# Strassen's form for the second product of a fused Fourier mixing and SoLU block, with its sums on GpSimd

## The chip, the core and the metric

The kernel runs on one core of a Trainium2 chip. Times are device microseconds (us) of one execution. The kernel before took 1793.22 us (median of four executions, 1790.22 to 1795.94; the prediction had the first three of them, with 1792.19). Traces come from one profiled execution each; every profiled run used here is of the state "fast", so no disturbed clock enters the comparison.

Engine names as the profile has them: PE is TensorE (matmuls), PEld its weight loads, DVE is VectorE, ACT is ScalarE, POOL is GpSimd, SP is SyncE, which here only issues transfers. A name such as L486 is a line of the kernel that the view belongs to; the same statement has another line number in another kernel.

## The reference, cut to what matters

```python
X = np.fft.rfft(x, axis=1)                       # x: (8, 3136, 256)
y = np.fft.irfft(X * (filt_r + 1j*filt_i)[None], n=3136, axis=1)
x = y.reshape(25088, 256)
h = x @ w_in                                     # 256 -> 1024
e = np.exp(h - h_max);  sm = e / (sum(e) + 1e-9)
solu = h * sm
ln = (solu - mu) / np.sqrt(var + 1e-6) * g_ln
out = ln @ w_out                                 # 1024 -> 256
```

The transform of 3136 points is done in matmuls (49 x 64 points with twiddles between). The 25088 tokens are 196 blocks of 128. The mean of `ln` is folded into `w_out`, and its division by the deviation becomes a scale per row at the very end.

## The kernel before: what the change and the argument touch

The loop makes one step for each block of 128 tokens; two steps are a pair of blocks. The first product `h = x @ w_in` is already in Strassen's form over a pair: seven products instead of eight, on 128x128 sums that GpSimd makes one pair ahead.

```python
def pair_sums(j):                                     # GpSimd, 128 x 128
    sums[j] = s = wk2.tile([P, 4, P], FP32, ...)      # two buffers
    # ... a11 to a22: the four 128x128 parts of the pair's input
    tt = nc.gpsimd.tensor_tensor
    tt(out=s[:, 0, :], in0=a21, in1=a22, op=ALU.add)
    tt(out=s[:, 1, :], in0=s[:, 0, :], in1=a11, op=ALU.subtract)
    tt(out=s[:, 2, :], in0=a11, in1=a21, op=ALU.subtract)
    tt(out=s[:, 3, :], in0=a12, in1=s[:, 1, :], op=ALU.subtract)

def normalize(k):                                     # VectorE, two inputs of 128 x 1024 in SBUF
    # ...
    nc.vector.scalar_tensor_tensor(out=solu, in0=e, scalar=rsum, in1=solu,
                                   op0=ALU.mult, op1=ALU.mult, accum_out=nmu)
    # ... then ScalarE squares it for the variance
```

The normalised block is transposed in 32x32 pieces on VectorE and regrouped by four DMAs (`solu_t<-turn`). The projection is plain: eight matmuls of 256 columns per block, then one scaled eviction by VectorE.

```python
def project(k, ps, half):
    # ...
    for f in range(KF // 2 * half, KF // 2 * half + KF // 2):
        nc.tensor.matmul(out=ps, lhsT=solu_ts[divmod(k, 4)][:, f, :], rhs=w_out_sb[:, f, :], ...)

def scale(k, ps):
    # ...
    nc.vector.tensor_scalar(out=ot, in0=ps, scalar1=rss[g][:, a:a + 1], scalar2=None, op0=ALU.mult)
    # ...
    nc.sync.dma_start(out=rows[a], in_=ot)
```

Beside the token work runs the transform of the later images: rows are loaded (`r`), a first matmul makes `pa`, ScalarE copies it to `t1`, which goes to DRAM as `d1`; it comes back as `t2`, is multiplied with the twiddle table and the filter (`pb`, `p`, `i`, `pc`, `g`), goes to DRAM as `d2`, comes back into the same row buffers `r` and gives `y` (`py`). In the trace `d<-t` is the store of `t1`, and `t<-d` is either of the two loads back. The buffers for this:

```python
pools = {name: pool(name + "1", bufs)
         for name, bufs in (("r", 4), ("t1", 2), ("t2", 3), ("p", 2), ("g", 2))}
# ...
# a row load is issued when the row buffer four loads back is free:
at = max(t - 3, row_loads[n - 4][0] if n >= 4 else -1)
```

## Time and profile before

| of the kernel before | value |
|---|---|
| median time | 1793.22 us |
| span of the profiled run, mean clock | 1795.5 us, 0.988 |
| TensorE busy, share | 1721.1 us, 96% |
| VectorE, ScalarE, GpSimd busy | 64%, 55%, 40% |
| two-input instruction of `normalize` | 196 x 1308 ns |
| 128x128 sums on GpSimd | 392 x 579 ns (median 458) |

The share of busy time is no measure of the room that is left, since records of pipelined matmuls overlap: those of the projection last 379 ns on average and start 216 ns apart. I therefore use one account throughout. Each TensorE record gets the spacing at which records of its shape follow one another when nothing is in the way: 429 ns for 512 columns, 216 for 256 and 110 for 98 (about their mean; the median is 112). Their sum is what TensorE needs; the span less that sum is stall, whatever its reason. A pair begins with its product 1 of the first layer. For the kernel before that is 1672.4 us needed and 123.1 us of stall. Of the stall, 78.1 us come before the first pair of blocks, 28.5 in pairs 0 to 18 (up to 520 us), 7.9 in pairs 18 to 97 and 8.6 at the end. From pair 18 on, this kernel has next to no room to give.

What TensorE waited for is in the view of waits of the profile of the kernel before, for PE alone; its columns are the waiting instruction, what released it, total us, number and longest:

```profile
PE pa L176 <- DMA x<-in_x_dram: 21.3, 9, 6.9
...
PE m L464 <- ACT h L474: 7.5, 5, 4.9
PE pb L205 <- DMA de<-de_tbl: 4.9, 5, 2.0
...
PE py L260 <- DMA t<-d: 1.6, 2, 0.8
...
PE py L260 <- ACT t L179: 0.9, 1, 0.9
PE po L549 <- DVE h L512: 0.8, 1, 0.8
```

And from the groups of its page, the two-input instruction of `normalize` (count, then busy us and mean ns, then idle time before it):

```profile
L512 DVE SCALAR_TENSOR_TENSOR h<-e,rsum,h 128x1024 f32<-128x1024 f32 x196 | 256.4, 1308 | 7.1 <-DMA x<-in_x_dram 0.3
```

No line names GpSimd (POOL); the only wait for VectorE which the list holds outside the transform is 0.8 us.

### The profile page before, as it was taken

How to read it: one execution, taken by the hardware profiler on the slowest of the kernel's cores; microseconds unless marked ns; L12 is line 12 of the kernel's file. 1: busy time of each engine (PE TensorE's matmuls, PEld its weight loads, DVE VectorE, ACT ScalarE, POOL GpSimd, SP SyncE). 2: the span in 40 equal slices, each digit the busy share in tenths (PEclk: the TensorE clock that was granted, in tenths of full speed). 3: DMA queues.
4: the chain of work that ended last, by engine and by line, in shares of the span. 5: the costliest groups of instructions: out<-in, count | busy, mean ns of one | idle time of the engine just before them, and what ended most of it. 6: DMA issues, size and time to landing. Idle time of an engine off the chain costs nothing.

```text
span 1795.5 us, 22752 instructions
## 1 busy us (share of the span) xinstructions
PE 1721.1 (96%) x6324; PEld 1112.1 (62%) x6324; DVE 1155.9 (64%) x2370; ACT 990.9 (55%) x1623; POOL 718.8 (40%) x1698
## 2 busy tenths in 40 slices
PE   6589889999999999999999999999999999999998
PEld 2125455566666666766666666676777677666666
DVE  0794545567666665677777655667676766677773
ACT  2265555566666655566666555555655555555452
POOL 3242544465455543335445333344443332324331
PEclk9699999999999999999999999999999999999999
DMA  9786789987799765577667565567775444433334
GB/s 270 250 258 191 217 224 247 246 215 205 207 232 222 191 184 145 151 167 199 180 174 203 142 162 146 127 170 191 191 188 133 107 120 108 107 103 104 102 96 119
DMA packets 323180, 313.98 MB, mean 175 GB/s; under 512 B 26465, under 2 KB 284514, under 8 KB 323056
## 3 DMA queue, kind: packets, MB, share of 16 engines
q1 hardware_dynamic: 292496, 219.79, 48.3%
q0 software_dynamic: 28768, 86.45, 16.6%
q10 hardware_dynamic: 1792, 6.29, 1.0%
q8 instruction: 53, 0.87, 0.2%
q14 instruction: 71, 0.58, 0.1%
HBM read 131.55 MB, written 81.40 MB: 119 GB/s over the span
## 4 chain that ended last, share of the span: by engine, by line
PE 83%; DMA 9%; DVE 3%; ACT 2%; issue 1%; POOL 1%; SPq 1%; DVEq 0%; ACTq 0%; POOLq 0%
PE po L549 35%; PE m L464 30%; PE py L260 6%; PE pa L176 4%; PE pc L235 4%; PE pb L205 4%; DMA x<-in_x_dram 3%; DMA d<-t 2%; DMA t<-d 2%; DMA de<-de_tbl 1%; DVE p L226 1%; DVE p L224 1%; PE idle L370 1%; DMA solu_t<-turn 0%; DVE i L225 0%
## 5 line engine op out<-in xcount | busy, mean ns | idle before, releaser
L549 PE MATMUL po<-w_out_sb,solu_t 128*128 128x256 f32 x3136 | 724.5, 379 | 2.4 <-DMA solu_t<-turn 1.6
L549 PEld LDWEIGHTS po<-w_out_sb,solu_t 128*128 128x128 f32 x3136 | 593.3, 190 | 190.0 <-issue 114.9
L464 PE MATMUL m<-w_in_sb,sums 128*128 128x512 f32 x784 | 399.1, 600 | 7.5 <-ACT h L474 7.5
L514 ACT ACTIVATE e<-h,nmu 128x1024 f32<-128x1024 f32 x196 | 225.1, 1149 | 223.3 <-DVE h L512 219.5
L464 PE MATMUL m<-w_in_sb,y 128*128 128x512 f32 x588 | 286.8, 597 | 0.1
L474 ACT COPY h<-m 128x512 f32<-128x512 f32 x294 | 172.4, 586 | 176.6 <-PE m L464 162.9
L512 DVE SCALAR_TENSOR_TENSOR h<-e,rsum,h 128x1024 f32<-128x1024 f32 x196 | 256.4, 1308 | 7.1 <-DMA x<-in_x_dram 0.3
L488 DVE CUSTOM_DVE_ANT_0 h<-m,h 128x512 f32<-128x512 f32 x196 | 133.9, 683 | 173.3 <-ACT h L474 86.0
L243 POOL DMA_DIRECT2D d<-g x101 | 77.2, 764 | 416.0 <-ACT g L238 407.0
L522 DVE STREAM_TRANSPOSE turn<-h 128x1024 f32<-128x1024 f32 x196 | 242.2, 1236 | 0.4 <-DVE ot L558 0.3
L496 ACT ACTIVATE e<-h,nmax 128x1024 f32<-128x1024 f32 x196 | 225.8, 1152 | 0.1
L558 DVE TENSOR_SCALAR ot<-po,rs_t 128x256 f32<-128x256 f32 x196 | 94.3, 481 | 171.6 <-issue 84.9
L464 PEld LDWEIGHTS m<-w_in_sb,sums 128*128 128x128 f32 x784 | 141.3, 190 | 96.0 <-issue 72.6
L541 POOL COPY rs_t<-rs 32x1 f32<-32x1 f32 x784 | 181.6, 232 | 35.7
L464 PEld LDWEIGHTS m<-w_in_sb,y 128*128 128x128 f32 x588 | 109.7, 191 | 112.7 <-issue 92.5
L224 DVE TENSOR_TENSOR p<-pb,f 128x512 f32<-128x512 f32 (+1 forms) x101 | 69.1, 685 | 149.9 <-ACT i L217 147.5
L176 PE MATMUL pa<-x,wf_t 98*100 98x512 f32 x256 | 138.3, 649 | 25.8 <-DMA x<-in_x_dram 21.3
L260 PEld LDWEIGHTS py<-wi_t,t 100*128 100x128 f32 x1024 | 131.7, 192 | 50.1 <-issue 31.5
L263 ACT COPY y<-py 128x392 f32<-128x392 f32 x128 | 108.2, 846 | 85.8 <-PE py L260 84.8
L179 ACT COPY t<-pa 100x512 f32<-100x512 f32 (+1 forms) x112 | 71.8, 646 | 133.5 <-PE pa L176 109.9
L260 PE MATMUL py<-wi_t,t 100*128 100x98 f32 x1024 | 132.0, 273 | 2.6 <-DMA t<-d 1.6
L205 PE MATMUL pb<-t,de 128*128 128x512 f32 (+1 forms) x250 | 108.1, 532 | 19.4 <-DMA t<-d 11.5
(65 smaller groups left out, 1441.4 us busy)
## 6 DMA issues: line engine op xcount, KB each, us to landing
solu_t<-turn SPq DMA_DIRECT2D x784, 128.0 KB
t<-d SPq DMA_DIRECT2D x99, 256.0 KB
d<-g POOLq DMA_DIRECT2D x99, 256.0 KB, 4.4
out_dram<-ot SPq DMA_DIRECT2D x196, 128.0 KB
x<-in_x_dram SPq DMA_DIRECT2D x64, 384.0 KB
t<-d SPq DMA_DIRECT2D x64, 384.0 KB
d<-t POOLq DMA_DIRECT2D x48, 384.0 KB, 5.8
f<-f_dram POOLq DMA_DIRECT2D x104, 128.0 KB, 5.7
```

The lines of the kernel that those rows point to most:

```text
L176: nc.tensor.matmul(out=ps[0:NK, j], lhsT=wf_t, rhs=self.xs[i][0:NR, 2 * u:2 * u + 2, :], start=True, stop=True)
L205: nc.tensor.matmul(out=ps[:, w * j:w * j + w, :], lhsT=self.des[i][:, j, 0, :], rhs=t2[:, w * j:w * j + w, :], start=True, stop=True)
L260: nc.tensor.matmul(out=psv[:, i, :], lhsT=t4s[e, ch][:, i, cb * P:cb * P + P], rhs=wi_t, start=True, stop=True)
L464: nc.tensor.matmul(out=ms[j, bank], lhsT=lhsT, rhs=w_in_sb[:, w, :], start=m in (1, 2, 7), stop=True, skip_group_check=True)
L474: nc.scalar.copy(out=h_half(k, i), in_=ms[j, 0])
L488: nc.vector.tensor_tensor_reduce(out=h_half(k, i), in0=ms[j, bank], in1=h_half(*kept), scale=1.0, scalar=sofar, op0=ALU.add, op1=ALU.min, ...
L496: nc.scalar.activation(out=e, in_=hs[k], func=AFT.Exp, bias=nmaxs.pop(k)[:, 1:2], scale=-1.0, accum_out=esum)
L512: nc.vector.scalar_tensor_tensor(out=solu, in0=e, scalar=rsum, in1=solu, op0=ALU.mult, op1=ALU.mult, accum_out=nmu)
L514: nc.scalar.activation(out=e, in_=solu, func=AFT.Square, bias=nmu, scale=-float(DFF), accum_out=variances[g][:, i:i + 1])
L522: nc.vector.transpose(out=turns[g][:, :, i, :], in_=solus.pop(k).rearrange("p (f j) -> p f j", j=32))
L541: nc.gpsimd.tensor_copy(out=rss[g][32 * i:32 * i + 32, c:c + 1], in_=rs[32 * c:32 * c + 32, i:i + 1])
L549: nc.tensor.matmul(out=ps, lhsT=solu_ts[divmod(k, 4)][:, f, :], rhs=w_out_sb[:, f, :], start=(f == 0), stop=(f == KF - 1), skip_group_chec ...
```

## The change

Its intent: the projection too is done for two blocks at once in Strassen's form. With the two blocks as rows and the halves of `DFF` as columns, seven products of four matmuls of 128 columns, 28 in all, take the place of 16 matmuls of 256 columns. The price is four sums of 128x512 per pair on GpSimd, and more, smaller evictions. Three things come with it: the weight combinations of `w_out` make that tile 14 KB per partition instead of 8, the sums need 8 KB more, and the buffers of the transform are cut by 10 KB to pay for it; loads of tables and spectrum rows move from SyncE's to ScalarE's queue; each row load is one transfer instead of two. Beside these, half of the tile of the small sums gets one buffer instead of two (`s23` in the kernel).

```diff
-LAG = 8
+LAG = 9
-    w_out_sb = consts.tile([P, KF, C], FP32, name="w_out_sb")
+    w_out_sb = consts.tile([P, 7, KF // 2, C // 2], FP32, name="w_out_sb")
...
-             for name, bufs in (("r", 4), ("t1", 2), ("t2", 3), ("p", 2), ("g", 2))}
+             for name, bufs in (("r", 3), ("t1", 3), ("t2", 2), ("p", 2), ("g", 2))}   # t1: half pieces
-        at = max(t - 3, row_loads[n - 4][0] if n >= 4 else -1)
+        at = max(t - 3, row_loads[n - 3][0] if n >= 3 else -1)
-            products[t].append(lambda sp=sp, i=i: sp.multiply(i))
+            products[t].append(lambda sp=sp, i=i: sp.multiply(i, bufs=1))               # one i tile
...
-            ahead(t, 3).append(lambda sp=sp, i=i: sp.fetch(i))
+            ahead(t, 2).append(lambda sp=sp, i=i: sp.fetch(i, nc.scalar.dma_start))
-        nc.sync.dma_start(out=de[:, 0:count], in_=de_dram[:, s:s + count, :, :])
+        nc.scalar.dma_start(out=de[:, 0:count], in_=de_dram[:, s:s + count, :, :])
...
+    def project_sums(p, step):
+        (a11, a12), (a21, a22) = solu_ts[p, 0], solu_ts[p, 1]
+        if step == 0:
+            s1 = upool.tile([P, KF // 2, P], FP32, name=f"u1_{p}", tag="u1")
+            sum_of(s1, a21, a22, ALU.add)
+            sum_of(a21, a11, a21, ALU.subtract)
+            solu_sums[p] = s1, None, a21, None
+        else:
+            s2 = spool.tile([P, KF // 2, P], FP32, name=f"u2_{p}", tag="u2")
+            s4 = spool.tile([P, KF // 2, P], FP32, name=f"u4_{p}", tag="u4")
...
+            sum_of(s2, s1, a11, ALU.subtract)
+            sum_of(s4, a12, s2, ALU.subtract)
...
+    def project(p, m):
...
+        for f in range(KF // 2):
+            nc.tensor.matmul(out=pos[p, bank], lhsT=lhs[:, f, :], rhs=w[:, f, :], ...)
...
...
+    def keep_out(p, i, to):          # ScalarE, scaled copy of a product that two outputs share
+    def finish_out(p, i, n, kept, bank):   # VectorE, 128 columns, adds the kept one
```

In the order of the step, `project_sums(j - 3, 0)` stands after products 3 and 4 of the first layer in odd steps, ahead of `pair_sums(j + 1)`; `project_sums(j - 4, 1)` stands in even steps.

## The prediction

The prediction's sum came to 1792 - 62 + 4.5 + 4 + 15 = 1754 us and was shaded to 1750. Cut is the reason given for a spacing of 112 ns where streaming alone would need 108; the spacing itself is measured, 112 ns for 98 columns in the kernel before and 112 for 128 columns in the changed one. In rival (a), 1722 is 1739 with 109 ns for each of the 5488 records instead of 112, an estimate from the eight records that took 0.87 us.

"The lock" is my assumption that VectorE's two-input instruction (L512) and a sum on GpSimd hold each other up. The lines quoted for it show a sum that took 1.11 us when it started under L512, and the next one 0.46.

> **What bounds the kernel now.** I read the page first (busy shares, chain that ended last, groups), then the stretches, then instructions in order of time. From the page:
>
> ```profile
> PE 1721.1 (96%) x6324; PEld 1112.1 (62%) x6324; DVE 1155.9 (64%) x2370; ACT 990.9 (55%) x1623; POOL 718.8 (40%) x1698
> ...
> PE 83%; DMA 9%; DVE 3%; ACT 2%; issue 1%; POOL 1%; SPq 1%; DVEq 0%; ACTq 0%; POOLq 0%
> PE po L549 35%; PE m L464 30%; PE py L260 6%; PE pa L176 4%; PE pc L235 4%; PE pb L205 4%; DMA x<-in_x_dram 3%; DMA d<-t 2%; DMA t<-d 2%; DMA de<-de_tbl 1%; DVE p L226 1%; DVE p L224 1%; PE idle L370 1%; DMA solu_t<-turn 0%; DVE i L225 0%
> ...
> L549 PE MATMUL po<-w_out_sb,solu_t 128*128 128x256 f32 x3136 | 724.5, 379 | 2.4 <-DMA solu_t<-turn 1.6
> ```
>
> TensorE bounds it, and the projection (L549) is the largest item on the chain. Its 3136 records are 196 blocks x 8 matmuls x 2: an fp32 matmul shows as two pairs of load and stream. Busy time of pipelined matmuls overlaps, so I take the spacing of starts instead. Stretches of the run show where TensorE is really full:
>
> ```profile
> 0.00:100.00 100.00, 63.65 (x101) 20.40 (x102) 44.76 (x78) 33.21 (x44) 32.27 (x55) 0.85 0.86 257
> 100.00:200.00 100.00, 87.66 (x306) 44.23 (x305) 62.16 (x117) 56.16 (x89) 36.32 (x58) 0.97 0.74 224
> 200.00:300.00 100.00, 86.56 (x285) 48.24 (x284) 56.07 (x117) 58.70 (x100) 47.85 (x104) 0.97 0.85 226
> ...
> 700.00:900.00 200.00, 200.00 (x764) 133.21 (x763) 139.03 (x285) 121.20 (x198) 84.24 (x205) 1.00 0.68 171
> ...
> 1600.00:1700.00 100.00, 100.00 (x354) 66.39 (x353) 71.22 (x154) 50.44 (x85) 34.89 (x101) 1.00 0.39 102
> ```
>
> Columns: length, busy of PE, PEld, DVE, ACT, POOL, clock, DMA share, GB/s. From about 400 us on TensorE has no gap; before 300 us it idles 12 to 36 us per 100 and the DMA engines are at 0.74 to 0.86 (0.94 between 300 and 400). The spacing:
>
> ```profile
> 900.66 3.62 PE L549 MATMUL po<-w_out_sb,solu_t 128*128 128x256 f32 x16
> 904.12 1.02 PE L464 MATMUL m<-w_in_sb,sums 128*128 128x512 f32 x2
> ...
> 916.15 1.03 PE L260 MATMUL py<-wi_t,t 100*128 100x98 f32 x8
> 917.02 1.05 PE L464 MATMUL m<-w_in_sb,sums 128*128 128x512 f32 x2
> ```
>
> Sixteen records of 256 columns take 904.12 - 900.66 = 3.46 us, 216 ns each; 512 columns cost 429 ns (median of 973 spacings of L464). Eight of 98 columns take 0.87 us, 109 ns each; inside such a run the median spacing is 112 ns, although 98 columns at 256 columns' rate would stream in 83 ns. [...] This line decides the worth of the change.
>
> [...] Our sums of 128 elements have a median of 458 ns[...]. [...]
>
> ```profile
> 1652.07 1.28 DVE L512 SCALAR_TENSOR_TENSOR h<-e,rsum,h 128x1024 f32<-128x1024 f32 x1
> ...
> 1652.56 1.11 POOL L451 TENSOR_TENSOR sums<-y 128x128 f32<-128x128 f32 x1 [3.15 <-PE m L464]
> ...
> 1653.75 0.46 POOL L452 TENSOR_TENSOR sums<-sums,y 128x128 f32<-128x128 f32 x1
> ```
>
> L451 started under L512, took 1.11 us, and the next sum 0.46. [...]
>
> **The change, part by part.**
> TensorE: 3136 x 216 ns = 677 us go. Added are 98 pairs x 7 products x 4 matmuls x 2 = 5488 records of 128 columns. Streaming alone would need about 108 ns[...]; I take 112: 615 us. Gain 62 us (0.64 per pair). Not the eighth (85 us) that seven for eight promises[...]. All lies on the path, except where DMA sets the pace: the trace has 14 of the 196 blocks projected before 400 us (one begins at 381.43, the next at 397.36 us), and their 14 x 0.32 = 4.5 us I count as lost.
> GpSimd: 392 sums of 128x512 x 1.27 us = 498 us, making 1217 of some 1740. Per pair of blocks 5.1 us come to 84.24/200 x 16.5 = 6.9 us in the middle and 34.89/100 x 13.06 = 4.6 us at the end (13.06 us is the spacing of pairs there). So 12.0 of 15.9 us, and 9.7 of 12.4. Waits for the lock come on top: two L512 per pair, 2.6 us at worst. Off the path on average, but 80 to 95% of it.
> VectorE: 196 x 481 ns = 94 us go; 392 PSUM operations of 128 columns, an estimate of 347 each from the 749 of L485's 512 and the 481 of L558's 256 columns: 136 us. Net +42, plus lock waits up to 1.27 us a time.
> ScalarE: 294 copies of 128 columns, 265 ns by the line through 586 (512) and 372 (256): 78 us; and some 152 issues of 0.42 us (what SyncE takes for them) = 64. It reaches 1133 us, no bound.
> SyncE: loses those issues and the second half of each row load. Its gain is order: loads no longer queue behind a store that waits (589 us of its waits are for L558).
> End: the last pair's sums lie bare, two steps of two, 5.1 us, less what the shorter products save: +4.
> Waits newly put on TensorE: in an odd step without spectral work, TensorE needs 3 x 0.86 + 4 x 0.90 = 6.2 us. VectorE and ScalarE have a chain beside it: product 5 read by the copy (1.6 us), exponential 1.34, copy of product 1 0.3, its finish 0.35, reciprocal 0.3, L512 1.37, L485 0.8: about 6.1 us before bank 0 is free. There is no slack there for a lock wait, where before bank 0 was freed about 0.9 us early (1654.0 against 1654.9). Where spectral work is mixed in there are 3 to 4 us more of TensorE per pair. I guess 0.15 us per pair, 15 us, as a choice and not a measurement.
> Sum: 1792 - 62 + 4.5 + 4 + 15 = 1754. The row loads' release, and that the buffers look sized to keep this going, make me shade it to 1750.
>
> **Rivals.**
> (a) No new wait: 1792 - 62 + 8.5 = 1739, or 1722[...]. For it: TensorE's waits for GpSimd's sums are near nothing today. Against: the 6.1 of 6.2 us above.
> (b) GpSimd or the lock becomes the bound: a sum of 1.27 us held against L512, and the loop from product 4 over the regroup DMA (4.5 us in the end stage), two sums, the pair's own sums and product 6. That loop is about 12 us at 12.4 a pair. With 0.6 us more in each pair the gain is gone: 1795. For it: sums of 128 elements already rise from 458 to a mean of 579. Against: more work per pair in most of the run.
> (c) The stage up to 400 us is bound by DMA, and [...]fewer row buffers (4 to 3) make it longer: +10 to 15, 1765.
> (d) The smaller matmuls cost more than 112 ns[...]: at 123 ns nothing is left, 1792 or more.
>
> **Range and chances.** Between (a) at its best and half of (b): 1722 to 1785. Faster by over 2% means below 1756; the centre is near the edge, so 0.56, 0.38 and 0.06.
>
> **What would show it.** In the changed kernel's trace: the spacing of 128-column matmuls (112 expected; 123 kills it); the median of the 128x512 sums (1.27 us) and their mean (up to 1.7 under the lock); GpSimd's share near 70%; TensorE's waits for outputs m and o on VectorE or ScalarE (15 us), for the sums (under 10), and for row loads before 400 us (up to 15 more); pairs in the end stage 12.4 to 12.7 us apart instead of 13.06. The prediction is wrong if that spacing stays above 12.9[...].

## The result

The changed kernel took 1822.07 us (median of four, 1820.77 to 1824.32). It computes the right result. Ratios in this document are the mean time of one kernel's fast runs over that of the other's fast runs of the same rounds, so not quite the ratio of the medians that are quoted; here the ratio is 1.0163, with a 95% interval of 1.0141 to 1.0184. That is slower by 1.6%, where 1750 us and a range of 1722 to 1785 had been predicted. (It is within 2% of the kernel before, the middle one of the prediction's three chances, 0.38.)

From the page of the changed kernel, first the busy shares and the chain that ended last, then groups (line, engine, operation, output<-inputs, shapes, count, then busy us and mean ns, then idle time before and what ended it):

```profile
PE 1686.6 (93%) x8692; PEld 1149.0 (63%) x8692; DVE 1246.2 (69%) x2586; ACT 1069.8 (59%) x1917; POOL 1267.2 (70%) x2090
...
PE 63%; DMA 10%; DVE 9%; POOL 6%; issue 6%; ACT 4%; SPq 1%; ACTq 1%; POOLq 0%; DVEq 0%
...
L595 PE MATMUL o<-w_out_sb,solu_t 128*128 128x128 f32 x3136 | 405.1, 278 | 5.0 <-DVE ot L614 4.0
...
L534 DVE SCALAR_TENSOR_TENSOR h<-e,rsum,h 128x1024 f32<-128x1024 f32 x196 | 292.2, 1491 | 7.1 <-DVE rsum L531 0.3
...
L465 POOL TENSOR_TENSOR solu_t<-solu_t,solu_t 128x512 f32<-128x512 f32 x98 | 156.7, 1599 | 7.7
```

TensorE fell from 83% of the chain to 63%, and VectorE, GpSimd and ScalarE rose together from 6% to 19%. The two-input instruction of `normalize`, whose code did not change, takes 1491 ns on average instead of 1308; its median is still 1286, so it is a minority of instances that became much longer: 79 of 196 are over 1350 ns, against 24 before.

The same stretches of the run as those of the prediction (length, then busy us of PE, PEld, DVE, ACT, POOL with counts, clock, DMA share, GB/s), changed kernel:

```profile
200.00:300.00 100.00, 77.95 (x253) 43.70 (x254) 51.51 (x111) 50.00 (x89) 53.85 (x101) 0.85 0.66 190
...
700.00:900.00 200.00, 190.22 (x1024) 131.89 (x1023) 141.25 (x295) 126.41 (x226) 145.76 (x248) 0.99 0.60 164
1600.00:1700.00 100.00, 97.59 (x558) 70.36 (x557) 76.89 (x175) 58.20 (x111) 80.97 (x133) 1.00 0.39 101
```

TensorE now has holes in the middle too, 190 of 200 us. Between 200 and 300 us it is less busy than before, its granted clock is 0.85 instead of 0.97, and the DMA engines fell from 0.85 to 0.66: this stretch is not held by the bandwidth of transfers. The waits below show transfers that start late.

In the account by stage, in us of stall (needed time 1672.4 before, 1609.8 after):

```text
stage              before   after   difference
before pair 0        78.1    78.2     +0.1
pairs 0 to 18        28.5    64.5    +36.0    the transform of later images is dense here
pairs 18 to 70        4.3    42.4    +38.1
pairs 70 to 97        3.6     8.1     +4.5    no transform left but the last step
end                   8.6    16.0     +7.4
sum                 123.1   209.2    +86.1
```

So the saving came: 1672.4 - 1609.8 = 62.6 us. It was eaten by 86.1 us of new stall, and 86.1 - 62.6 = 23.5 us is the difference of the spans (1819.0 - 1795.5). What ended TensorE's waits, in the view of waits of the changed kernel for PE:

```profile
PE py L266 <- ACT t L185: 17.0, 4, 7.9
...
PE pb L210 <- DVE p L230: 11.8, 13, 2.9
...
PE m L486 <- DVE nmax L510: 10.6, 13, 2.8
PE pb L210 <- DMA de<-de_tbl: 9.7, 4, 3.2
...
PE m L486 <- POOL s L465: 6.9, 9, 1.4
PE o L595 <- ACT ot L607: 5.2, 8, 1.4
PE o L595 <- DVE ot L614: 4.0, 4, 1.7
```

There are two kinds. The first line is the early stage: four long waits of `py`, between 174 and 290 us. Most of the others are short waits for VectorE and for GpSimd's sums, the larger part of them after pair 18.

**The short waits.** Two extracts of the changed kernel's timeline (start, duration, engine, line, operation; in brackets the idle time before and what ended it), the first in the early stage, the second near the end:

```profile
245.42 3.31 DVE L534 SCALAR_TENSOR_TENSOR h<-e,rsum,h 128x1024 f32<-128x1024 f32 x1
246.36 1.28 POOL L465 TENSOR_TENSOR u<-u,solu_t 128x512 f32<-128x512 f32 x1
247.71 2.14 POOL L465 TENSOR_TENSOR u<-solu_t,u 128x512 f32<-128x512 f32 x1
...
248.83 1.15 ACT L536 ACTIVATE e<-h,nmu 128x1024 f32<-128x1024 f32 x1 [3.83 <-DVE h L534]
```

```profile
1644.72 1.28 DVE L534 SCALAR_TENSOR_TENSOR h<-e,rsum,h 128x1024 f32<-128x1024 f32 x1
1644.84 2.30 POOL L465 TENSOR_TENSOR u<-solu_t,u 128x512 f32<-128x512 f32 x1
...
1650.72 1.13 PE L486 MATMUL m<-w_in_sb,s 128*128 128x512 f32 x2 [0.81 <-POOL s L465]
...
1651.01 1.56 DVE L534 SCALAR_TENSOR_TENSOR h<-e,rsum,h 128x1024 f32<-128x1024 f32 x1
```

In the first, VectorE's instruction of 1.28 us takes 3.31. A sum of 1.28 us runs inside it. If VectorE stood still for all of that, which is my reading and not shown, 0.75 of the 2.03 us more stay unexplained (in its first 0.93 us GpSimd was issuing transfers). The next sum then starts under VectorE and takes 2.14. In the second VectorE was first, and the sum takes 2.30 us. Six us later a product of the first layer waits for the small sums, which stand behind the long ones in GpSimd's queue. Each of the two lengthens the other's work: 3.31 us for 1.28 on VectorE, 2.14 and 2.30 for 1.28 on GpSimd.

**The long waits.** In the timeline of the changed kernel between 282 and 292 us:

```profile
282.28 1.69 POOL L190 DMA_DIRECT2D d<-t  x3
...
289.45 0.59 ACT L185 COPY t<-pa 100x512 f32<-100x512 f32 x1 [10.17 <-DMA d<-t]
290.09 2.03 PE L266 MATMUL py<-wi_t,t 100*128 100x98 f32 x8 [7.93 <-ACT t L185]
...
291.91 3.65 PE L595 MATMUL o<-w_out_sb,solu_t 128*128 128x128 f32 x16
```

ScalarE cannot copy the next `pa`, since all its `t1` buffers wait for stores that GpSimd issued late; it stands 10.17 us, and TensorE, whose output bank (the store of sums that its products write to) ScalarE should empty, 7.93. Of the 10.17 us, some 3 pass before GpSimd issues the stores at 282.28, behind its sums. Afterwards eight matmuls of 98 columns take 2.03 us, where the prediction's lines showed eight in 1.03, and sixteen of 128 columns take 3.65 instead of 1.95. TensorE's granted clock, 1.00 from 270 to 285 us, stands at 0.50 from 285.3 to 295.3 us. The same is seen earlier: after a pause of 2.59 us `py` takes 3.73 us for 16 records, at a granted clock of 0.50 from 216.9 to 227.1 us, where the kernel before took 2.03 after a pause of 0.89. If the pause brings the clock down, it is paid twice; that is my reading of these two places, and no run tests it. In pairs 0 to 18 the granted clock is at half for 6.8 us before and 43.9 us after. Counting records at one and a half to 2.3 times their spacing as half clocked, the lost time in the whole run is an estimate of 22 to 25 us before and 39 to 51 after, by which records are counted; this is a part of the stall above, not more of it.

### The profile page after: what moved, and what is told of

Its sections match the earlier page's. It is cut to its first block, busy times and chain, and to the rows that moved or that the text cites. A ratio compares the mean times of both kernels' runs of the same rounds, so it can differ in the third digit from the quotient of the medians.

```text
span 1819.0 us, 29269 instructions
## 1 busy us (share of the span) xinstructions
PE 1686.6 (93%) x8692; PEld 1149.0 (63%) x8692; DVE 1246.2 (69%) x2586; ACT 1069.8 (59%) x1917; POOL 1267.2 (70%) x2090
## 4 chain that ended last, share of the span: by engine, by line
PE 63%; DMA 10%; DVE 9%; POOL 6%; issue 6%; ACT 4%; SPq 1%; ACTq 1%; POOLq 0%; DVEq 0%
PE o L595 24%; PE m L486 22%; PE py L266 6%; PE pa L183 3%; PE pb L210 3%; PE pc L241 3%; DVE h L534 2%; DMA de<-de_tbl 2%; DMA d<-t 2%; DMA x<-in_x_dram 2%; DMA solu_t<-turn 2%; POOL rs_t L566 2%; POOL u L465 1%; DMA t<-d 1%; DVE turn L544 1%
## 5 line engine op out<-in xcount | busy, mean ns | idle before, releaser
L486 PE MATMUL m<-w_in_sb,s 128*128 128x512 f32 x784 | 400.7, 603 | 18.4 <-ACT h L496 11.4
L595 PE MATMUL o<-w_out_sb,solu_t 128*128 128x128 f32 x3136 | 405.1, 278 | 5.0 <-DVE ot L614 4.0
L595 PEld LDWEIGHTS o<-w_out_sb,solu_t 128*128 128x128 f32 x3136 | 385.1, 195 | 35.8 <-issue 27.5
L595 PEld LDWEIGHTS o<-w_out_sb,u 128*128 128x128 f32 x2352 | 308.4, 192 | 144.6 <-issue 114.5
L595 PE MATMUL o<-w_out_sb,u 128*128 128x128 f32 x2352 | 312.6, 276 | 6.9 <-ACT ot L607 5.2
L534 DVE SCALAR_TENSOR_TENSOR h<-e,rsum,h 128x1024 f32<-128x1024 f32 x196 | 292.2, 1491 | 7.1 <-DVE rsum L531 0.3
L465 POOL TENSOR_TENSOR u<-solu_t 128x512 f32<-128x512 f32 x98 | 142.4, 1453 | 154.9 <-DMA solu_t<-turn 95.6
L614 DVE SCALAR_TENSOR_TENSOR ot<-o,rs_t,ot 128x128 f32<-128x128 f32 x294 | 101.3, 345 | 212.5 <-ACT ot L607 157.4
L465 POOL TENSOR_TENSOR u<-solu_t,u 128x512 f32<-128x512 f32 x98 | 150.7, 1537 | 59.6 <-PE o L595 54.7
L486 PEld LDWEIGHTS m<-w_in_sb,s 128*128 128x128 f32 x784 | 130.5, 193 | 96.4 <-issue 69.0
L465 POOL TENSOR_TENSOR solu_t<-solu_t,solu_t 128x512 f32<-128x512 f32 x98 | 156.7, 1599 | 7.7
```

The lines of the kernel that those rows point to most:

```text
L465: nc.gpsimd.tensor_tensor(out=out, in0=in0, in1=in1, op=op)
L486: nc.tensor.matmul(out=ms[j, bank], lhsT=lhsT, rhs=w_in_sb[:, w, :], start=m in (1, 2, 7), stop=True, skip_group_check=True)
L595: nc.tensor.matmul(out=pos[p, bank], lhsT=lhs[:, f, :], rhs=w[:, f, :], start=f == 0 and m in (1, 2, 7), stop=True, skip_group_check=True)
```

## The experiments

My theory after the traces had two parts. For pairs 18 to 97, GpSimd's sums and VectorE's two-input instructions hold each other up, as in the two extracts above (the lock, in what follows; the expectations say exclusion), and the chain from VectorE to TensorE has no slack for that. For pairs 0 to 18, the new order of work or the buffers that were given up hold the transform. Rivals: the time that the sums take in GpSimd's queue; the smaller matmuls and evictions themselves; the moved loads.

Eighteen kernels were run. Every run was also timed against the kernel before, whose medians were 1798.1, 1794.6, 1796.1, 1797.8 and 1795.4. A table of all of them stands after the last. Kernels that read something other than the sums give a wrong result; that is said with each.

### The sums: removed, unread, without reads, elsewhere

**No sums.** The products read the transposed blocks themselves (a wrong result).

```diff
 def project_sums(p, step):
     (a11, a12), (a21, a22) = solu_ts[p, 0], solu_ts[p, 1]
     if step == 0:
-        ...four sums
+        solu_sums[p] = a21, a11, a21, a12
```

> The changed kernel without the 392 sums of solu on GpSimd (the products read the unsummed halves, so the result is wrong on purpose). By my accounting TensorE's added stall over the kernel before is 86 us: 36 in the first 18 pairs, 44 in pairs 18 to 97, 7 in the tail. Theory 'sums' (the sums on GpSimd delay VectorE and through it TensorE): the 44 and most of the tail go, 1770 to 1778 us. Rival 'buffers and loads' (smaller buffers, ScalarE's queue, one-piece row loads): 1812 us or more.

Measured: 1811.37 us, ratio 1.0064 (1.0023 to 1.0104). VectorE's instruction went back to 1307 ns and the stall of pairs 70 to 97 from 8.1 to 0.2 us, but the stall of pairs 0 to 18 stayed (68.4 against 64.5). The expectation missed by over 30 us, and the time is within 1 us of what was given for the rival: whatever holds the early stage is not cured by taking the sums away. The name of its wait changed. Of `py`'s waits in pairs 0 to 18, those for ScalarE's copy fell from 13.4 to 3.5 us, and those for the loads of rows rose from none to 17.5; in the waits of PE over the whole run:

```profile
PE py L266 <- DMA t<-d: 25.0, 6, 15.4
```

**Sums made, but not read** (wrong). GpSimd makes sums of the same size in the same places (the second one goes over `s1` instead of `a21`, so that the block is not spoiled), and the products read the blocks themselves, so no product waits for a large sum.

```diff
+            sum_of(s1, a21, a22, ALU.add); sum_of(s1, a11, a21, ALU.subtract)
+            solu_sums[p] = a21, a11, a21, a12
```

> The sums are all computed on GpSimd in the same places and of the same size, but TensorE's products don't read them (wrong result on purpose). If the exclusion between GpSimd's reads and VectorE's two-input instructions is what costs, this stays near the changed kernel: 1808 to 1822 us, and the mean of the 128x1024 normalising instruction stays near 1490 ns. If TensorE's waits for the sums themselves cost (the loop over regroup, sums, product), it falls to the run without sums, about 1775 us.

Measured: 1863.71 us, 1.0375 (1.0313 to 1.0438): slower than the changed kernel, and outside both of the expected values. VectorE's instruction stayed long (1505 ns), so the lock works whether or not the sums are read. But something new appeared, in the waits of PE:

```profile
PE m L487 <- POOL s L466: 33.5, 30, 3.3
```

The small sums of the first layer wait in GpSimd's queue behind the large ones, which in turn wait for the regroup DMA (174.7 us of GpSimd's time, against 95.6 in the changed kernel). With no product to wait for the sums, TensorE runs on and meets the late small sums instead. This reading is from the trace alone. The experiment therefore doesn't give the price of the lock; the next does.

**Sums as memsets.** Each sum becomes two memsets of the same tile (wrong). They write as much and wait for the same buffers, but read nothing from SBUF.

```diff
+    def blank(out):
+        for value in (0.25, 0.5):
+            nc.gpsimd.memset(out, value)
-            sum_of(s1, a21, a22, ALU.add)
+            blank(s1)                              # and so for all four
```

> Each sum is replaced by two memsets of the same 128x512 tile on GpSimd: TensorE still waits for GpSimd and GpSimd is still busy, but it reads no SBUF (wrong result on purpose). If the exclusion costs: the normalising instruction falls from 1490 to near 1300 ns and the time to 1775 to 1785 us. If GpSimd's occupancy or TensorE's wait for it costs: 1808 us or more, provided two memsets take near the 1.27 us of a sum.

Measured: 1781.8 us, 0.9926 (0.988 to 0.9973), the first version that beats the kernel before. In the groups of this kernel, VectorE's instruction and GpSimd's memsets:

```profile
L534 DVE SCALAR_TENSOR_TENSOR h<-e,rsum,h 128x1024 f32<-128x1024 f32 x196 | 253.2, 1292 | 7.1 <-DVE rsum L531 0.3
```

```profile
L571 POOL MEMSET u<- 128x512 f32 x588 | 304.1, 527 | 141.0 <-PE o L599 121.2
...
L571 POOL MEMSET solu_t<- 128x512 f32 x196 | 102.6, 524 | 172.2 <-DMA solu_t<-turn 93.4 <-PE m L486 29.7 <-PE o L599 26.1
```

A pair of memsets lasts 1.05 us against the 1.28 of an undisturbed sum, and GpSimd still waits 93.4 us for the regroup DMA, as it did 95.6. What is gone is the reading, and some of the time: the memsets occupy GpSimd for 407 us, the sums for 583. VectorE's instruction is at 1292 ns and the stall fell from 209.2 to 171.0 us, by 38: 10.8 in pairs 0 to 18 and 27.9 in pairs 18 to 97. With the reads gone, on the same engine and in the same order, VectorE's instruction isn't lengthened: 1292 ns, against 1491 in the changed kernel and 1505 with the sums unread.

Is all of the 38 us the lock's? The run without sums has no lock either, and its stall fell by only 7.2. The waits in pairs 18 to 70 reconcile the two. TensorE's waits for VectorE there (`m`, `o` and `pb` together) fell from 18.6 us to 6.4 with memsets and to 7.0 without sums; but `py`'s waits for rows rose from 2.5 to 7.5 without sums, and only to 3.7 with memsets. So some 12 us of waits in this stage went with the lock in both runs. The rest of the 38 cannot be put down to the lock alone: the memsets are also shorter, and in the last pairs the order of GpSimd's queue was the cause, as a run below shows.

**Sums on VectorE** (right result).

```diff
-            sum_of(s1, a21, a22, ALU.add)
+            nc.vector.tensor_tensor(out=s1, in0=a21, in1=a22, op=ALU.add)      # all four
```

> The sums on VectorE instead of GpSimd (right result). 392 x 0.69 us = 270 us more VectorE work in place of the waits for the exclusion. If what costs is the exclusion, this is no better by itself, since VectorE's own work grows more (by 2.8 us per pair) than the waits shrink (about 1.5 us per pair): 1825 to 1860 us. If GpSimd's in-order queue (DMA issues behind the sums) were the cause, it would be faster: below 1800 us.

Measured: 1996.7 us, 1.1124 (1.1082 to 1.1165), far above the expected 1825 to 1860 (whose 0.69 us a sum is what VectorE's two-input instructions of 128x512 take in the kernel before, 682 to 691 ns). TensorE's main wait became the evictions that stand behind the sums on VectorE, `m` for VectorE's `h`, 70.6 us. VectorE was busy for 1420 us of 1994.5. An engine that isn't full can still be the wrong place, if its work is in the chain that frees TensorE's banks.

### The early stage: which buffers

**After's buffer counts in the kernel before.** No Strassen, no sums, no moved loads; only rows 3 instead of 4, `t1` as three half pieces that are stored one by one, `t2` 2 instead of 3, one `i` tile, and the loads' places in the order that go with these counts (right result).

```diff
-             for name, bufs in (("r", 4), ("t1", 2), ("t2", 3), ("p", 2), ("g", 2))}
+             for name, bufs in (("r", 3), ("t1", 3), ("t2", 2), ("p", 2), ("g", 2))}
-                name=f"i_{self.n}_{i}", tag="i")
+                name=f"i_{self.n}_{i}", tag="i", bufs=2 if self.n == 0 else 1)
-            ahead(t, 3).append(lambda sp=sp, i=i: sp.fetch(i))
+            ahead(t, 2).append(lambda sp=sp, i=i: sp.fetch(i))
-        at = max(t - 3, row_loads[n - 4][0] if n >= 4 else -1)
+        at = max(t - 3, row_loads[n - 3][0] if n >= 3 else -1)
...
```

> The kernel before (direct projection) with only the changed kernel's buffer counts in the transform stages: three half-piece buffers for two whole ones, row buffers 3 for 4, spectrum rows 2 for 3, one for two of the turned products, and the fetches moved accordingly (right result). Theory 'few buffers': it loses the 20 to 36 us that the changed kernel stalls more in the first 18 pairs: 1812 to 1830 us. Rival: the early loss comes with the new projection, LAG or loads: 1800 us or less.

Measured: 1833.34 us, 1.0204 (1.0177 to 1.0231). With none of the rest of the change, the buffers alone cost the kernel before 36 us of stall (158.9 against 123.1), of which 28.7 in pairs 0 to 18 and 7.8 in pairs 18 to 70. So they are enough to cost what the changed kernel lost early. That the changed kernel lost it through them is a further step; the last two runs below bear on it.

**Three row buffers alone**, and **the half pieces alone**, both in the kernel before (right results).

```diff
# three row buffers
-             (("r", 4), ("t1", 2), ...
+             (("r", 3), ("t1", 2), ...
-        at = max(t - 3, row_loads[n - 4][0] if n >= 4 else -1)
+        at = max(t - 3, row_loads[n - 3][0] if n >= 3 else -1)
# half pieces: first step stored in two halves from three buffers of half the size
-             (("r", 4), ("t1", 2), ...
+             (("r", 4), ("t1", 3), ...
```

> The kernel before with three row buffers instead of four and nothing else (right result). The buffers together cost it 36 us. If row buffers are the larger part: 1813 to 1825 us. If not: 1805 us or less.

> The kernel before with three half-piece result buffers instead of two whole ones, each half stored on its own, and nothing else (right result). If these are the larger part of the 36 us: 1813 to 1825 us. If not: 1805 us or less.

Measured: 1818.33 us, 1.0126 (1.0092 to 1.0159), and 1802.67 us, 1.0036 (1.0005 to 1.0067): row buffers are the larger part. The stall of pairs 0 to 18 rose from 28.5 to 52.7 with three row buffers and to 34.4 with the half pieces. Of the 28.7 us of the whole set, the row buffer has 24.2 and the half pieces 5.9 (the sum is a little over). The 7.8 us of pairs 18 to 70 come with neither (4.2 and 4.6, where the kernel before has 4.3); the counts of `t2` and `i`, which are left, were not run alone. The waits of PE with three row buffers show what a row buffer is for:

```profile
PE pa L176 <- DMA x<-in_x_dram: 30.0, 11, 9.8
PE py L260 <- DMA t<-d: 12.7, 1, 12.7
```

Both had been 21.3 and 1.6 us. With three buffers a load is issued one load later, and the rows come late.

**A shared ring of five** half pieces and `g` tiles in the changed kernel, in place of three and two apart, at the same memory (right result).

```diff
-             for name, bufs in (("r", 3), ("t1", 3), ("t2", 2), ("p", 2), ("g", 2))}
+             for name, bufs in (("r", 3), ("t1", 5), ("t2", 2), ("p", 2))}
+    pools["g"] = pools["t1"]
```

> The changed kernel with the three half-piece buffers of the first transform's results and the two of the inverse's results put into one ring of five (same memory, right result). Theory 'few buffers': in the first 18 pairs ScalarE waits for a store of such a half piece to land (34 us in all, up to 10.2 us at a time), TensorE waits for ScalarE and then runs at half clock; with five buffers the early stall of 64 us falls to 35 to 45 and the time to 1795 to 1805 us. Rival 'the loads set the early pace': no change, 1817 us or more.

Measured: 1819.05 us, 1.011 (1.0046 to 1.0174), as the rival had it; the four executions lie between 1799.56 and 1825.56. The long wait for ScalarE went, and another came in the same place. In the waits of PE of this kernel, in place of the 17.0 us for ScalarE's `t`:

```profile
PE py L267 <- DMA t<-d: 17.8, 4, 12.2
```

**Stores of the first step issued at once by ScalarE** instead of late by GpSimd (right result).

```diff
-                stores[t].append(lambda ...: sp.store_first(i, 2 * u, nc.gpsimd.dma_start))
+                # in the same job as the copy:
+                sp.first(i, (u,), ...), sp.store_first(i, 2 * u, nc.scalar.dma_start)
```

> The changed kernel with each half piece of the first transform's results stored from ScalarE's queue right after ScalarE's copy, not from GpSimd's queue at the end of the step (right result). If the stores standing behind GpSimd's sums and small copies cost (a wait of 10.2 us on one store at 289 us), the early stall falls from 64 to 40 to 48 us and the time by 15 to 25 us, to 1797 to 1807 us. If the buffers alone do it: 1815 us or more.

Measured: 1828.9 us, 1.0169 (1.0127 to 1.0211). Again the wait for ScalarE's copy shrank (13.4 to 3.1 us in pairs 0 to 6), and the wait for `t<-d` took its place (none to 12.9). Two different cures of the wait that the trace showed both failed the same way. The wait named by the trace was the first of two in a row. The second is the load of rows, which a missing row buffer delays, as the kernel before with three of them shows. The run without sums fits this: there GpSimd is free to store early, and the wait for rows appears (17.5 us).

**The loads undone.** Tables and spectrum rows on SyncE's queue again, row loads in two transfers (right result).

```diff
-            ahead(t, 2).append(lambda sp=sp, i=i: sp.fetch(i, nc.scalar.dma_start))
+            ahead(t, 2).append(lambda sp=sp, i=i: sp.fetch(i, nc.sync.dma_start))
-            row_loads.append((t, lambda sp=sp, i=i: sp.fetch_x(i, whole)))
+            row_loads.append((t, lambda sp=sp, i=i: sp.fetch_x(i)))
```

> The changed kernel with spectrum rows and tables loaded from SyncE's queue again and row loads split in two again (right result). Theory 'the new loads cost early': [...]ScalarE's issues delay the first 18 pairs; undone, 1800 to 1810 us. Rival 'they were needed': loads then queue behind stores and regroups that wait, 1830 us or more.

Measured: 1836.58 us, 1.0213 (1.0178 to 1.0249), 9 us worse than with them by the ratios and 15 by the medians. This part of the change does its work; it isn't where the time went.

### Repairs of order

**The small sums first** in GpSimd's queue, ahead of the large ones (right result).

```diff
+            if hid and j + 1 < pairs:
+                pair_sums(j + 1)
             if 0 <= j - 3 < pairs:
                 project_sums(j - 3, 0)
...
-                if j + 1 < pairs:
-                    pair_sums(j + 1)
```

> GpSimd's four small sums for the next pair's hidden products are put in front of the first two sums of solu instead of behind them (right result). If the in-order queue costs (small sums stand behind sums that wait for the regroup transfer), TensorE's waits for the small sums (7 to 10 us) go, and what VectorE does after them comes earlier: 1805 to 1813 us. If the exclusion alone costs, no change: 1817 to 1825 us.

Measured: 1819.43 us, 1.0133 (1.0099 to 1.0166). Pairs 70 to 97 were cured (8.1 to 0.9 us of stall), which shows that the order in GpSimd's queue was the cause there. The last 13 pairs, which have no transform, show it best. In the changed kernel their spacing alternates between 12.26 and 13.33 us: in every second pair GpSimd has 16 small copies to make (32x1, a median of 179 ns and a mean of 225), and in the pair after it the small sums come late and a product waits 0.80 us for them. The second extract above shows one of these waits; there are six of them, and TensorE has no other wait in these pairs. With the small sums first it has none, and all 13 pairs take 12.26 to 12.31 us. The lock is still at work: of the 26 instances of VectorE's instruction in these pairs six are lengthened by 0.27 to 0.29 us, where the changed kernel has seven and the memsets none. So in pairs without transform there is slack for a lengthening of this size.

Pairs 18 to 70 became worse (42.4 to 55.2): TensorE's waits for VectorE rose from 18.6 to 31.9 us there, although VectorE's instruction was lengthened less (a mean of 1463 ns against 1529). My reading, which no run tests, is that the large sums now start later and meet VectorE's instructions elsewhere: a change of order moves the meeting and doesn't remove it.

**Large sums in two halves** (128x256; their median is 728 ns), and **ScalarE's copy of the output bank after product 6 ahead of the square** (both right results).

```diff
-        nc.gpsimd.tensor_tensor(out=out, in0=in0, in1=in1, op=op)
+        for n in range(parts):       # halves
...
+            nc.gpsimd.tensor_tensor(out=a, in0=b, in1=c, op=op)
# the other kernel
                 project(p, 6)
+                keep_out(p, 1, (1, 0))
                 project(p, 7)
...
-            if proj:
-                keep_out(p, 1, (1, 0))
```

> The changed kernel with each 128x512 sum on GpSimd cut into two of 128x256 (right result). If VectorE's waits behind a sum are what delays TensorE in pairs 30 to 97 (38 + 8 us of stall), [...]the mean of the normalising instruction falls from 1491 to 1400 ns or less and the time by 8 to 15 us, to 1805 to 1813 us. If GpSimd's own occupancy is what costs, 392 more instructions of 0.19 us make it slower: 1825 us or more.

> ScalarE's copy of product 6 out of its bank stands in front of the square instead of behind it (right result). If ScalarE standing still before the square for the delayed normalising instruction (343 us of idle there) is how VectorE's delay reaches TensorE's output banks, the waits of TensorE and VectorE on that copy shrink: 1800 to 1814 us. If those waits have slack: 1817 to 1825 us.

Measured: 1815.78 us, 1.0131 (1.0066 to 1.0195), and 1821.17 us, 1.0138 (1.0104 to 1.0171). Neither differs from the changed kernel by more than its interval. With halves the mean of VectorE's instruction fell to 1447 ns and not below 1400; two halves take 2 x 728 - 1277 = 179 ns more than one whole sum.

**Four row buffers by making the fourth sum in place.** To save a tile, the fourth sum is written over `a12` after product 2 has read it; with a shared ring of four that pays for the row buffer (right result). The second kernel joins the three small repairs to it.

```diff
-            s4 = spool.tile([P, KF // 2, P], FP32, name=f"u4_{p}", tag="u4")
-            sum_of(s4, a12, s2, ALU.subtract)
+    def last_sum(p):                 # called between products 2 and 6
+        sum_of(a12, a12, s2, ALU.subtract)
-             (("r", 3), ("t1", 3), ("t2", 2), ("p", 2), ("g", 2))
+             (("r", 4), ("t1", 4), ("t2", 2), ("p", 2))          # t1 and g share
```

> The fourth row buffer is bought back: the fourth sum is written over the half it is taken from, the transform's results and the inverse's share a ring of four (right result; the sum's place in GpSimd's order moves by half a step). Theory 'few row buffers': the early stall (64 us in pairs 0 to 18, 28 in the kernel before) falls to 35 to 45 us, the time to 1792 to 1805 us. Rival: the early stall is set by the stores or the loads' form: 1815 us or more.

> Row buffers as in the run before this one, plus the small sums first, halved sums and the early copy (right result). If early buffers, the in-order queue and the exclusion are separate costs that add up, about 25 + 8 + 12 + 5 us come off the changed kernel's 1820: 1765 to 1785 us, below the kernel before. If they hide one another: 1790 us or more.

Measured: 1949.86 us, 1.085 (1.0793 to 1.0906), and 1854.81 us, 1.0315 (1.0276 to 1.0354). The moved sum waits for product 2 at the head of GpSimd's queue, and everything behind it waits too. In the waits of PE of the first of them:

```profile
PE m L488 <- POOL s L467: 99.7, 51, 5.0
```

The time therefore says nothing about row buffers, but it shows what an in-order queue does with one instruction that isn't ready. The waits tell why it gained nothing early: in pairs 0 to 18 of these two kernels `py` still waited 11.1 and 12.6 us for ScalarE's copy, the first of the two waits. The kernels that cured this one had three row buffers and waited for rows instead: 14.0 us with the ring, 14.0 with stores at once, 13.8 in the next run. No kernel with a right result had both cures.

**Four repairs that cost no memory together**: stores from ScalarE, the shared ring, small sums first, sums in halves (right result).

```diff
+ ring of five, pair_sums ahead of project_sums, sums in halves
-                stores[t].append(lambda ...: sp.store_first(i, 2 * u, nc.gpsimd.dma_start))
+                stores[t].append(lambda ...: sp.store_first(i, 2 * u, nc.scalar.dma_start))
-            stores[t + 1].append(lambda ...: sp.store(i, nc.gpsimd.dma_start))
+            stores[t + 1].append(lambda ...: sp.store(i, nc.scalar.dma_start))
```

> The changed kernel with all stores of the transforms from ScalarE's queue, the ring of five buffers, the small sums first and halved sums (right result). If the early stores, the in-order queue and the exclusion are separate: 1822 less 20, 8 and 8 us is 1780 to 1795 us, level with or just below the kernel before. If they hide one another: 1805 us or more.

Measured: 1828.46 us, 1.0185 (1.0137 to 1.0233). The repairs didn't add up.

### Both causes taken away at once

**No sums, and the buffers given back** (wrong): the 8 KB of the sums' tiles pay for four row buffers, four half pieces and two `i` tiles. **Memsets of one small tile, and four row buffers and half pieces** (wrong): GpSimd is kept busy, but reads nothing and takes only 2 KB.

```diff
# both
-             (("r", 3), ("t1", 3), ("t2", 2), ("p", 2), ("g", 2))
+             (("r", 4), ("t1", 4), ("t2", 2), ("p", 2), ("g", 2))
-        at = max(t - 3, row_loads[n - 3][0] if n >= 3 else -1)
+        at = max(t - 3, row_loads[n - 4][0] if n >= 4 else -1)
# the first: no sums, sp.multiply(i);   the second, for each two sums:
+        for _ in range(2):
+            blank(blank_t)
```

> No sums (wrong result on purpose, the products read the transposed blocks themselves), and with the 8 KB that frees: four row buffers, four half pieces for the transform's first step and two turned tiles again, as before the change. It takes both causes away at once. My theory (memory for the early stage, lock and GpSimd's queue for the rest): the early stall of pairs 0 to 18 falls from 68 us without the sums to 30 to 40, the middle stays near the 32 of the run without sums, and the time is 1770 to 1780. If the early stall comes from the sums' order or from smaller products alone, and not from memory, it stays above 60 and the time at 1805 to 1815.

> Each sum becomes two memsets of one small tile that nothing reads (GpSimd keeps about its length, SBUF reads and the added tiles go; wrong result on purpose), with four row buffers and four half pieces again. My theory: VectorE's two-input instruction stays at 1.29 us, the early stall is 30 to 40 instead of 54, the middle near 20, and the time is 1755 to 1770, which is what the prediction's case without new waits meant (1739) plus a tail of its own. Rival, that GpSimd's occupied time and its queue are the cost: the time stays near the 1782 of the memsets without the buffers, or above.

Measured: 1776.58 us, 0.9882 (0.9836 to 0.9927), and 1772.64 us, 0.9869 (0.9838 to 0.99). The first is as expected in its total, but not in its parts: the early stall is 45.4 us instead of 30 to 40, and the middle fell from 31.6 to 20.6 instead of staying near 32. The second is 3 us above the expected range, with 43.2 early instead of 30 to 40; 5 us of its total are before the first pair, a stretch that varies as much between other runs for no reason in the change. In pairs 0 to 18 both of `py`'s waits are now short together: 6.7 us for rows and 2.6 for ScalarE's copy in the first, 3.7 and 3.7 in the second. From 1811.37 to 1776.58 the same kernel without sums gained 35 us (33 by the ratios) by the buffers alone.

That bears on what the change is worth at best. With both causes gone, the stall is 163 us and not 123. Against the kernel before, the memset version still has 14.7 more in pairs 0 to 18, 13.7 in 18 to 70, 10.5 at the end and 5.2 at the start, less 3.8 in 70 to 97: 40.3 us. No run divides this rest. It lies in what both kernels still have of the change: the order of products, the smaller evictions, the moved loads, `t2` at two. So a version of this change free of lock and of the cut buffers would, by an estimate from these two wrong results, stand near 1773 us, and not at 1750.

All runs by stage, stall in us of the profiled run (median of all runs of a kernel in the last column):

```text
kernel                       start  0-18  18-70  70-97   end    sum   median
before                        78.1  28.5    4.3    3.6   8.6  123.1  1793.22
changed                       78.2  64.5   42.4    8.1  16.0  209.2  1822.07
no sums                       83.4  68.4   31.6    0.2  18.4  202.0  1811.37
sums unread                   77.8  66.6   62.0   26.3  19.2  252.0  1863.71
sums as memsets               77.8  53.7   22.8   -0.2  16.9  171.0  1781.80
sums on VectorE               82.0  91.8  140.2   47.9  22.9  384.8  1996.70
ring of five                  81.6  61.4   45.3    8.4  16.1  212.8  1819.05
small sums first              83.2  58.5   55.2    0.9  17.4  215.2  1819.43
loads undone                  78.7  71.3   49.3    7.6  17.5  224.5  1836.58
sums in halves                79.9  58.3   39.5    9.9  17.9  205.4  1815.78
copy ahead of square          78.1  55.4   49.9    7.5  15.5  206.4  1821.17
stores at once                74.0  65.9   54.8    7.3  16.1  218.1  1828.90
fourth sum in place, 4 rows   78.1  63.8   82.0   68.9  40.4  333.3  1949.86
the same, with repairs        77.7  56.7   56.2   23.5  33.8  247.8  1854.81
four repairs, 3 rows          74.1  69.7   57.8    0.4  16.9  218.8  1828.46
no sums, buffers back         77.9  45.4   20.6    0.2  18.5  162.6  1776.58
memsets, buffers back         83.3  43.2   18.0   -0.2  19.1  163.4  1772.64
before, changed's buffers     78.3  57.2   12.1    3.6   7.7  158.9  1833.34
before, 3 rows                79.8  52.7    4.2    3.6   8.3  148.6  1818.33
before, half pieces           78.6  34.4    4.6    3.6   7.5  128.7  1802.67
```

Each row is one profiled run; differences of a few us between rows are not to be read.

## Why the prediction was wrong, by its own steps

- **TensorE's saving: right.** 62 us predicted, 62.6 in the account. Records of 128 columns follow one another at a median of 112 ns, as assumed. Rival (d), matmuls dearer than 112 ns, didn't happen.
- **The sums' length and GpSimd's share: right.** The median of the 128x512 sums is 1277 ns against the 1.27 us that was reckoned with, and GpSimd is busy for 70%, as said. The mean is 1486 ns, within the "up to 1.7" that was named. VectorE's finishes took 345 ns (347 estimated). ScalarE's copies took 362 ns where the line through two sizes gave 265; nothing hung on that.
- **"I guess 0.15 us per pair, 15 us": this step failed, in size and in place.** The new stall in pairs 18 to 97 is 38.1 + 4.5 = 42.6 us, 0.54 us per pair of these 79. The prediction saw no slack in a step without spectral work (6.1 of 6.2 us) and 3 to 4 us more room where spectral work is mixed in. The runs show the reverse. In the pairs without spectral work, with the small sums first, lengthenings of up to 0.29 us cost TensorE no wait; what cost there was the order of GpSimd's queue. Of the 42.6 us, 38.1 lie in pairs 18 to 70, where the transform runs; 12 us of waits for VectorE there went with the lock. The lock, shown in the prediction with its own lines, had been put into "up to 1.27 us a time" and never multiplied: VectorE's excess over 1285 ns in this instruction grew from 4.6 to 40.4 us. Even without the lock 9.9 us (memsets, buffers back) to 14.7 us (memsets alone) of new stall remain after pair 18. That this is near the guessed 15 is luck, since the guess was to cover the lock too.
- **"+4.5" for the early stage: this step failed.** The prediction took the early stage as one in which a saving is merely lost. The stall grew by 36.0 us there. The cause was named in rival (c), fewer row buffers, but sized at 10 to 15 us together with the form of the row loads, given as one of four rivals, and not put into the sum. Instead the sum was shaded down by 4 us, because "the buffers look sized to keep this going". The changed kernel's buffer counts in the kernel before cost 36 us over the whole run, 28.7 in this stage, most of it by the fourth row buffer (24.2). What rival (c) gave as the mechanism beside it, a DMA stage that is full, is refuted for the worst stretch: the DMA share fell from 0.85 to 0.66 between 200 and 300 us. Row loads in one transfer were not tested alone; undoing them with the other moved loads made the kernel slower (1836.58 us). In the changed kernel giving the buffers back is worth 10.5 us (memsets) to 23.0 us (no sums) of the early stall.
- **"+4" at the end: right in kind.** It was +7.4.
- **Rival (b), GpSimd or the lock as the bound, 1795: the nearest.** Both of its causes are there, the lock in pairs 18 to 70 and GpSimd's order in the last pairs. Its size, 0.6 us per pair, is close to the mean of 0.54 found after pair 18, but not to the parts (0.73 in pairs 18 to 70, 0.17 after), so the number is partly luck. It did not have the early stage, and that is the distance to 1822.
- **The tests named in advance.** Spacing of 112 ns, the sums and GpSimd's share came out as said. TensorE's waits for the small sums (6.9 us) stayed under 10. The spacing of pairs in the end stage, "12.4 to 12.7 instead of 13.06", did not quite: in the last 13 pairs it is 13.06 throughout in the kernel before and 12.76 on average in the changed one, seven of them at 12.26 and six at 13.33. Its own limit of 12.9 was not crossed. The free pair is 0.80 us shorter, more than the 0.64 of the saving; in every second pair GpSimd's queue takes it back.
- **A slip in the working.** GpSimd at "80 to 95%" of the path does not follow from the two sums before it: 12.0 of 15.9 and 9.7 of 12.4 us are 75 and 78%, and with the whole 2.6 us of lock 92 and 99%. The page has it busy for 70%, but its queue was late in every second pair of the end all the same.

Together: the memsets gave back 38 us, the buffers cost 36 in the kernel before, and the end is 7, of 86. The two large ones overlap, and taking both away gave back 46 us and not 74; so the parts may not be added. With no sums the buffers are worth 39 us of stall, and with the memsets 8 (13 without the start, which happened to be 5.5 us longer in that run).

What stays open: how the remaining 40 us divide between the smaller evictions, the order of products, the moved loads and the `t2` buffer; how much of the memsets' 38 us is due to their being shorter than sums; why small sums first made pairs 18 to 70 worse; and whether a right version with four row buffers and early stores would reach the 1773 us. I found no place for the 4 KB without a new wait. No version with a right result beat the kernel before.

## What to carry to other kernels

When a change pays for itself with buffers, price the buffers first and alone: the old kernel with the new buffer counts is a small experiment (two lines for the row buffer, which has most of it), and here it would have shown a cost of 36 us against a saving of 62 before a line of the new algorithm was written. An engine with 60% of its time free isn't free for an instruction that lengthens another engine's (1308 to 1491 ns here), nor for one that stands in its queue before a small one that is needed soon (0.80 us of TensorE in every second pair of the end): multiply the lock by its count, write down the order of the queue, and ask in which stage TensorE has room for either. And where a trace names one wait, ask what stands right behind it, since curing the first may only bring up the second.
